# The last transform stage of a GFNet and MLP kernel: from 128-row groups to four quarters of the array

## The chip, the cores and the metric

The kernel runs on one core of a Trainium2 chip. The metric is the device time of that core in microseconds (us). A core has a matrix engine (PE, with its weight loads shown apart as PEld), a vector engine (DVE), a scalar engine (ACT), GpSimd (POOL), and SyncE (SP), which here issues most of the DMAs. PE reads both operands from SBUF and writes PSUM; a PSUM bank holds 512 fp32 values for each of 128 partitions.

## The reference

A Fourier mixing layer along the sequence, then an MLP with a hard-swish.

```python
X = np.fft.rfft(x, axis=1)                 # x: 8 x 3008 x 256
Y = X * (filt_r + 1j * filt_i)[None, :, :]
y = np.fft.irfft(Y, n=3008, axis=1)        # 24064 tokens of 256 channels in all
h = y @ w_in                               # 256 x 2048
g = h * np.clip(h + 3.0, 0.0, 6.0) / 6.0
out = g @ w_out                            # 2048 x 256
```

## The kernel before

**The transforms.** 3008 is 47 x 64, and each transform is done in two stages with the small tables of sines and cosines as matrix operands. For one batch element the units are: a_unit (47-point stage, stores to z_tmp), b_unit (64-point stage), f_unit and y_unit (multiplication by the filter, on DVE), bi_unit (inverse 64-point stage, stored to g_tmp by g_store), and the last stage, n_unit, which makes tokens out of g_tmp. The last stage writes channels on partitions and tokens along the free axis into `xn`, a ring of 768 token pairs, from which the MLP reads.

**The last stage.** Tokens come in pairs: from the real part of g_tmp comes the even sum (c = 0), from the imaginary part the odd sum (c = 1), and the two tokens of a pair are their sum and difference. For column j of the 64, the 47 even sums are a product over 48 rows (24 frequencies, twice: hh = 0 and 1), and so are the 47 odd sums. Columns are taken in chunks of NJ = 5, and there are 46 such chunks of full size over the 8 batch elements; columns 0 and 1 and the tail go in smaller ones. Before the change, the 5 x 48 = 240 rows of a chunk are stacked on 128 partitions in two layers of 128 and 112 rows, `t4[row, layer]`, and the table `groups` is block-structured to match: each layer multiplies 128 or 112 rows by 141 columns (three columns' worth, zero where a row isn't concerned), and the overlapping column of the two layers is summed in PSUM. `n_unit(i, dh)` does one 128-channel half dh of chunk i: four matmuls of 128 channels x 141 columns into one PSUM bank (L625), and one ACT copy into the ring (L641), two where the ring wraps. The unit is called twice a chunk, for dh = 0 and 1, in the same step or in two.

**Its loads.** `t4_load(i)` (L594) brings a chunk from g_tmp with SP: for each of five columns and two hh one DMA of 24 rows x 2 parts x 256 channels, one of them split at partition 128: 11 DMAs. `t4` has two slots of four layers, used in turn.

**The MLP.** It works on blocks of 512 tokens (256 pairs), 47 of them, with 8 steps a block (p = 0 to 7, 256 hidden units each), by a fast matrix multiplication with seven products instead of eight, in both matrices. One step holds 14 PE records of 256 columns (L690, up) and 28 of 128 columns (L766, down).

**What sets the order.** The order is written out by hand. The loop at the end walks over all steps. In each it issues up_1 (three products), then the early units planned for that step (`do(True)`: a_unit, b_unit, bi_unit, n_unit), then the rest of the MLP step, then the other planned work (`do(False)`: loads, stores, DVE work of the transforms). `plan` is filled by `at(step, fn, ...)`: the transforms of batch element n are spread over the blocks before the one where n begins, and each of these blocks has a kind, "c", "a", "A" or "B", by what it holds: a_units at steps 2, 4, 7 (c) and 1, 3, 5, 6, 7 (a); b_units at 2, 6 (A) and 4 (B); bi_units at 1 (c and the second A) and 0, 6 (B). `N_AT` gives for each kind the steps of the two n_units of a chunk that stands alone in its block, and of the first and second chunk where there are two. A chunk's load is planned one step after the second unit of the chunk before last.

**Banks.** a_unit, b_unit, bi_unit and n_unit draw their PSUM tiles from one pool of two banks, tag "f" (psF). a_unit, b_unit and bi_unit take both; an n_unit takes one. a_unit is also the model for what follows: it multiplies 47 rows by 64 columns on four quarters of the array, the two row halves (h) into a bank each, the two column halves (g) into 64 partitions each.

Of the kernel before, what the change touches and what calls it, by code (L numbers as in the profile page):

```python
# [10 lines left out]
FP32 = mybir.dt.float32  # L11
I32 = mybir.dt.int32
AXT = mybir.ActivationFunctionType
# [14 lines left out]
NA = 47  # L28
NC = 64
KH = 24  # L30
X0, XR = 16, 112
NF = N // 2 + 1
P = 128
D = 256
B = 8
DFF = 2048
HALF = 64
HC = NC // 2
# [9 lines left out]
TOK = 2 * NA  # L48
BLK = 512
NBLK = B * N // BLK  # L50
NJ = 5
PAIRS = BLK // 2
RING = 3 * PAIRS
ND = (NJ + 1) * TOK
NX = PAIRS - NJ * NA
NG = (HC - 2) // NJ
ATOM = 2 * KH
SPAN = 3 * NA
FIRST = tuple(range(NJ + 1, 0, -1))
LAST = NBLK - 1  # L60
CUT = NJ * 5 * NA + NA
# [17 lines left out]
def _make_tables():  # L79
    a = np.arange(NA)  # L80
    c = np.arange(NC)
    wa = np.zeros((P, HC * 2 * KH + 16))
    start = np.zeros((P, 2 * P))
    for h in range(2):
        for k in range(KH):
            th = 2 * np.pi * ((a * k) % NA) / NA

            at = k // 4 * 4 + (0, 2, 1, 3)[k % 4]
# [10 lines left out]
    for k in range(KH):  # L99
        for q in range(64):  # L100
            f, sign = (k + NA * q, 1.0) if q < 32 else (NA * (q - 31) - k, -1.0)
# [7 lines left out]
    for q in range(64):  # L109
        g, sign = (q, 1.0) if q < 32 else (31 - q, -1.0)  # L110
# [5 lines left out]
        at = g % 2 * 32 + (q // 2 if q < 32 else 16 + (q - 32) // 2)  # L116
# [8 lines left out]
        for h in range(2):  # L125
            s = -1.0 if h and g % 2 else 1.0
# [22 lines left out]

    rows = np.vectorize(row, excluded=(0, 1))  # L150
    late_rows = np.vectorize(late_row, excluded=(0, 1))
    groups = np.zeros((P, NG, 2, SPAN))
    ones = np.zeros((P, 2, TOK))
    first = np.zeros((P, NJ + 1, TOK))
    last = np.zeros((P, NJ + 1, TOK))
# [1 line left out]
    for k in range(KH):  # L157
        for j in range(HC):
            for (ri, hh), x in terms(k, j, rows).items():
                if j in FIRST:  # L160
                    first[hh * 64 + ri * 32 + k, FIRST.index(j)] = first_of(x, FIRST.index(j))
                if j < 2:
                    ones[ri * ATOM + hh * KH + k, j] = cs_of(x)
            if j in FIRST:
                for (ri, hh), x in terms(k, j, late_rows).items():
                    last[ri * ATOM + hh * KH + k, FIRST.index(j)] = cs_of(x)
            if j > 1:
                g, q = divmod(j - 2, NJ)
                c, s = (terms(k, j, rows)[0, hh][0] for hh in range(2))
                for hh, v in enumerate((c, s)):  # L170
                    t, p = divmod((NJ - 1 - q) * ATOM + hh * KH + k, P)
                    o = (NJ - 1 - q) * NA - t * 2 * NA
                    groups[p, g, t, o:o + NA] = v
        if k >= KH - TC:
            for q in range(64):
                fr = k + NA * q if q < 32 else NA * (q - 31) - k
                for n, j in enumerate(FIRST):
                    th = [2 * np.pi * ((fr * rows(j, h, a)) % N) / N for h in range(2)]
                    direct[q, k - KH + TC, n * TOK:(n + 1) * TOK] = 2 / N * first_of(np.cos(th), n)
                    direct[HALF + q, k - KH + TC, n * TOK:(n + 1) * TOK] = -2 / N * first_of(np.sin(th), n)  # L180
    wai = np.concatenate([t.reshape(P, -1) for t in (groups, ones, first, last)], axis=1)
    f = np.float32
# [4 lines left out]
def kernel(  # L187
# [9 lines left out]
    nc = tc.nc  # L197
# [12 lines left out]
    g_d = nc.dram_tensor("g_tmp", (B, NC, 2, KH, D), FP32, kind="Internal").ap()  # L210
# [6 lines left out]
    const = pool("const", 1)  # L217
# [14 lines left out]

    wa = const.tile([P, HC * 2 * KH + 16], FP32, name="wa")
    wf = const.tile([P, 4, 64], FP32, name="wf")
    NW = NG * 2 * SPAN + 2 * TOK
    wai = const.tile([P, NW], FP32, name="wai")
    groups = wai[:, 0:NG * 2 * SPAN].rearrange("p (g s n) -> p g s n", g=NG, s=2)
    ones = wai[:, NG * 2 * SPAN:].rearrange("p (s n) -> p s n", s=2)
    edge = wai[:, ds(2 * 2 * SPAN, ND)]
    edges = edge.rearrange("p (j n) -> p j n", n=TOK)  # L240
    wi = const.tile([P, 4, NC], FP32, name="wi")
    xs = const.tile([P, 3, XC, D], FP32, name="xs")
    ft = [const.tile([P, TC, D], FP32, name="ft%d" % i) for i in range(FB)]
    t4 = const.tile([P, 8, D], FP32, name="t4")
    xn = const.tile([P, 2, 2, RING], FP32, name="xn")
    w_all = const.tile([P, NP, 2, 7, P], FP32, name="w_all")
    w_in, w_out = ([w_all[:, p, i, :, :] for p in range(NP)] for i in range(2))
# [335 lines left out]
    def pair(i):  # L583
        b, js, o, n = chunks[i]
        return b * HC * NA + o, n
# [7 lines left out]

    def t4_load(i):  # L594
        b, js, _, _ = chunks[i]
        s0 = i % 2 * 4
        if len(js) < NJ:
            for q, j in enumerate(js):
                for hh in range(2):
                    for ri in range(2):  # L600
                        nc.sync.dma_start(t4[ds(ri * ATOM + hh * KH, KH), s0 + q, :], g_d[b, hh * HC + j, ri, :, :])
            return
        both = t4[:, ds(s0, 4), :].rearrange("p (c s) d -> p s c d", c=2)
        for q, j in enumerate(js):
            for hh in range(2):
                r, k = q * ATOM + hh * KH, 0
                while k < KH:
                    s_, p0 = divmod(r + k, P)
                    m = min(KH - k, P - p0)
                    nc.sync.dma_start(both[p0:p0 + m, s_, :, :],  # L610
                                      g_d[b, hh * HC + j, :, k:k + m, :].rearrange("ri k d -> k ri d"))
                    k += m

    ROWS = (P, NJ * ATOM - P)

    def n_unit(i, dh):
        ps = psF.tile([P, 512], FP32, name="psn", tag="f")
        b, js, o, n = chunks[i]
        s0 = i % 2 * 4
        t = b * HC * NA  # L620
        if len(js) == NJ:
            for c in range(2):
                for s_ in range(2):
                    r = ROWS[s_]
                    nc.tensor.matmul(ps[:, ds(c * NJ * NA + s_ * 2 * NA, SPAN)], t4[0:r, s0 + 2 * c + s_, ts(dh, P)],  # L625
                                     groups[0:r, (js[-1] - 2) // NJ, s_, :], start=c == 0 and s_ == 0, stop=True,
                                     skip_group_check=True)
            pieces = [(0, n, o, ps[:, 0:2 * n])]
        else:
            for q, j in enumerate(js):  # L630
                w = edges[0:2 * ATOM, FIRST.index(j), :] if i >= TAIL and j else ones[0:2 * ATOM, j, :]
                nc.tensor.matmul(ps[:, ts(q, TOK)], t4[0:2 * ATOM, s0 + q, ts(dh, P)], w, start=True, stop=True)  # L632
            pieces = [(a, m, to, ps[:, ts(q, TOK)])
                      for q, a, m, to in TO.get(i, [(q, 0, NA, o + q * NA) for q in range(len(js))])]
        for a, m_, to, src in pieces:
            src = src.rearrange("p (c n) -> p c n", c=2)
            done = 0
            while done < m_:
                r = (t + to + done) % RING
                m = min(m_ - done, RING - r)  # L640
                nc.scalar.activation(out=xn[:, dh, :, ds(r, m)], in_=src[:, :, ds(a + done, m)], func=AXT.Copy)  # L641
                done += m
        t += o
        if dh and (t + n) // PAIRS > t // PAIRS > 0:
            t_sums(t // PAIRS)


    def direct(i):
# [30 lines left out]
    def t_sums(k):  # L679
        t = xtp.tile([P, 5, PAIRS], FP32, name="xt")  # L680
        c0, s0, c1, s1 = (xb(k, d, c) for d in range(2) for c in range(2))
        u, v = (t[:, i, :] for i in (F5, F3))
        f1, f2, f3, f4, f5 = (t[:, i, :] for i in (F1, F2, F3, F4, F5))
        for o, x0, x1, op_ in ((f1, c0, s0, ALU.subtract), (u, c0, c1, ALU.add), (v, s0, s1, ALU.add),
                               (f4, u, v, ALU.subtract), (f5, u, v, ALU.add), (f2, c1, s1, ALU.add), (f3, f1, f2, ALU.add)):
            nc.gpsimd.tensor_tensor(out=o, in0=x0, in1=x1, op=op_)  # L686
        st["xt", k] = t
# [205 lines left out]
    plan = {}  # L893


    EARLY = (a_unit, b_unit, bi_unit, n_unit)

    def at(step, fn, *a):
        plan.setdefault((step, fn in EARLY), []).append((fn, a))

    with tc.manual_schedule():
# [126 lines left out]
                kinds[first[n] - 7 + d] = kind  # L1028

        N_AT = {"c": ((6, 6), (3, 3), (6, 6)), "a": ((2, 4), (2, 4), (6, 6)), "A": ((4, 5), (1, 1), (4, 5)), "B": ((2, 3), (1, 1), (2, 3))}  # L1030
        N_FIRST = {0: ((3, 4),), 1: ((), (2, 2), (3, 3)), 2: ((1, 1),), 3: ((1, 1),)}
        in_block = {}
        for i in range(2, len(chunks)):
# [2 lines left out]
        for i in range(2, len(chunks)):  # L1036
            k = pair(i)[0] // PAIRS
            head = chunks[i][2] == 0
            same = in_block[k]
            steps = (N_FIRST.get(k - 1) or N_AT[kinds.get(k - 1, "a")])[same.index(i) + 1 if len(same) > 1 else 0]  # L1040
            if head and len(same) == 1:
                steps = (6, 6)
            s0, s1 = ((k - 1) * NP + s for s in steps)
            n_at[i] = s1
            if head:
                stored = s0 - 3 + (k == first[1])
            at(max(stored, n_at[i - 2] + 1), t4_load, i)
            at(s0, n_unit, i, 0)
            at(s1, n_unit, i, 1)

# [136 lines left out]
```

## Time and profile before

| what | value |
|---|---|
| median of 3 runs | 2681.38 us (2681.22 to 2682.51) |
| the profiled execution: its own time | 2680.88 us |
| its span | 2679.1 us |
| granted TensorE clock | 1.00 of full speed |
| PE matmul records of L625 (n_unit, full chunks) | 736, mean 283 ns |
| ACT copies of L641, 128 x 470 | 62, mean 565 ns |
| DMAs of t4_load, 48 KB | 414 of the 418 in their group |

An fp32 matmul leaves two load records and two matmul records in the trace. "128\*128 128x141" means a stationary operand of 128 rows and 128 columns and a moving operand of 141 columns. Matmul durations reach from the start to a modelled end and overlap, so what a record costs is read from the distance between starts. A load (PEld) runs beside the matmul before it. In an instruction group, the figures after the bar are busy time and mean duration, and then the idle time of the engine just before them. In a list of waits, the figures are the total in us, the number of times, and the longest.

### The profile page before, as it was taken

Reading aid. Unit: us, or ns where it says so; the run is one execution under the profiler, and the core shown is the slowest. Engines: PE = TensorE matmul, PEld = TensorE weight load, DVE = VectorE, ACT = ScalarE, POOL = GpSimd, SP = SyncE. Lnnn points to the kernel's source line nnn. Section 1 sums busy time; section 2 is a strip of 40 time slices with the busy share of each in tenths; the row PEclk is TensorE's granted clock in tenths of the full one; section 3 lists DMA queues with packets and bytes.
Section 4 is the critical chain, followed back from the end, with each engine's and each line's share of the span. In section 5 each row is a group of like instructions: output and inputs, shape, how many; then the busy total and the mean of one; then the engine's idle time right before and its main releaser. Section 6 shows DMA issues by size and latency. Waiting matters only on the chain.

```text
span 2679.1 us, 48744 instructions
## 1 busy us (share of the span) xinstructions
PE 2661.1 (99%) x18640; PEld 2351.6 (88%) x18640; DVE 2069.1 (77%) x3503; ACT 1311.9 (49%) x2672; POOL 493.0 (18%) x731
## 2 busy tenths in 40 slices
PE   9999999999999999999999999999999999999999
PEld 6588898888988889888888888888888888899998
DVE  7878867887678876888777887788777878767666
ACT  3454454445444455445544545445454454554554
POOL 2251122111221112211121111211112111111110
PEclk9999999999999999999999999999999999999999
DMA  9632233212332123411233212231122321110000
GB/s 244 211 100 70 56 101 105 63 36 63 91 104 63 40 63 88 110 56 40 68 85 108 56 41 73 79 108 56 42 71 80 108 58 42 50 42 18 23 20 24
DMA packets 138663, 198.02 MB, mean 74 GB/s; under 512 B 27010, under 2 KB 102880, under 8 KB 138238
## 3 DMA queue, kind: packets, MB, share of 16 engines
q1 hardware_dynamic: 120901, 150.23, 19.6%
q0 software_dynamic: 16960, 44.16, 6.3%
q8 instruction: 148, 2.42, 0.4%
q14 instruction: 85, 0.70, 0.1%
q10 hardware_dynamic: 569, 0.50, 0.1%
HBM read 122.53 MB, written 83.98 MB: 77 GB/s over the span
## 4 chain that ended last, share of the span: by engine, by line
PE 94%; DVE 3%; DMA 2%; POOL 0%; issue 0%; ACT 0%; SPq 0%; POOLq 0%; DVEq 0%; ACTq 0%
PE po L766 43%; PE al L690 23%; PE be L690 17%; PE psn L625 3%; PE psf L543 2%; PE psf L452 2%; PE psf L499 1%; DVE g L740 1%; DMA g_tmp<-t 0%; DMA ft<-in_filt_i_dram 0%; DVE y L337 0%; DVE w_all L358 0%; DVE y L355 0%; PE psn L632 0%; DMA wa<-wb_t 0%
## 5 line engine op out<-in xcount | busy, mean ns | idle before, releaser
L766 PEld LDWEIGHTS po<-w_all,g 128*128 128x128 f32 x10276 | 1360.6, 191 | 149.1 <-issue 46.1
L766 PE MATMUL po<-w_all,g 128*128 128x128 f32 x10276 | 1397.6, 276 | 0.1
L735 ACT ACTIVATE r<-h,half_c 128x512 f32<-128x512 f32 x736 | 531.0, 721 | 342.3 <-DVE h L716 330.3
L740 DVE SCALAR_TENSOR_TENSOR g<-r,h 128x512 f32<-128x512 f32 x736 | 530.5, 721 | 198.0 <-ACT r L735 184.5
L690 PE MATMUL al<-xt,w_all 128*128 128x256 f32 x2208 | 659.9, 381 | 2.7 <-ACT s L701 1.4
L690 PE MATMUL be<-xt,w_all 128*128 128x256 f32 x1472 | 437.8, 379 | 0.0
L716 DVE TENSOR_TENSOR h<-be,s 128x512 f32<-128x512 f32 x368 | 253.8, 690 | 170.7 <-PE be L690 165.8
L690 PEld LDWEIGHTS al<-xt,w_all 128*128 128x128 f32 x2208 | 335.2, 192 | 4.5 <-ACT s L701 2.1
L690 PEld LDWEIGHTS be<-xt,w_all 128*128 128x128 f32 x1472 | 279.7, 190 | 37.9
L730 ACT ACTIVATE h<-al 128x256 f32<-128x256 f32 x368 | 141.3, 384 | 333.3 <-PE al L690 333.3
L721 DVE TENSOR_TENSOR h<-al,s 128x256 f32<-128x256 f32 x368 | 156.0, 424 | 157.7 <-PE al L690 156.5
L686 POOL TENSOR_TENSOR xt<-xn 128x256 f32<-128x256 f32 x184 | 153.8, 847 | 661.7 <-ACT xn L641 633.2
L748 DVE TENSOR_TENSOR g<-g 128x512 f32<-128x512 f32 x367 | 255.7, 697 | 12.6
L711 ACT ACTIVATE s<-al 128x256 f32<-128x256 f32 x368 | 141.4, 384 | 200.7 <-PE al L690 198.8
L702 ACT ACTIVATE s<-be 128x256 f32<-128x256 f32 x368 | 141.4, 384 | 174.6 <-PE be L690 174.6
L690 PE MATMUL al<-xn,w_all 128*128 128x256 f32 x736 | 220.8, 382 | 0.7 <-DVE h L721 0.6
L690 PE MATMUL be<-xn,w_all 128*128 128x256 f32 x736 | 219.0, 379 | 0.0
L750 DVE TENSOR_TENSOR g<-g 128x256 f32<-128x256 f32 x367 | 175.3, 478 | 12.5
L701 ACT ACTIVATE s<-al 128x256 f32<-128x256 f32 x368 | 141.2, 384 | 67.0 <-PE al L690 67.0
L747 DVE TENSOR_TENSOR g<-g 128x256 f32<-128x256 f32 x367 | 157.5, 429 | 12.5
L473 POOL DMA_DIRECT2D z_tmp<-t x192 | 95.1, 503 | 384.9 <-DVE t L466 366.8
L690 PEld LDWEIGHTS be<-xn,w_all 128*128 128x128 f32 x736 | 139.8, 190 | 19.1 <-DVE g L740 0.2
(149 smaller groups left out, 1844.0 us busy)
## 6 DMA issues: line engine op xcount, KB each, us to landing
g_tmp<-t POOLq DMA_DIRECT2D x96, 256.0 KB, 3.8
t<-z_tmp SPq DMA_DIRECT2D x42, 512.0 KB
t<-g_tmp SPq DMA_DIRECT2D x418, 48.0 KB
z_tmp<-t POOLq DMA_DIRECT2D x192, 96.0 KB, 2.6
xs<-in_x_dram SPq DMA_DIRECT2D x112, 128.0 KB
o_tmp<-o SPq DMA_DIRECT2D x46, 256.0 KB
ft<-in_filt_r_dram SPq DMA_DIRECT2D x168, 64.0 KB
ft<-in_filt_i_dram SPq DMA_DIRECT2D x168, 64.0 KB
```

The source lines that it names most:

```text
L686: nc.gpsimd.tensor_tensor(out=o, in0=x0, in1=x1, op=op_)
L690: nc.tensor.matmul(ps, w_in[p][:, w, :], x, start=start, stop=stop, skip_group_check=True)
L702: nc.scalar.activation(out=s5, in_=be[:, 1, :], func=AXT.Copy)
L711: nc.scalar.activation(out=s[:, 1, :], in_=al, func=AXT.Copy)
L716: nc.vector.tensor_tensor(out=st["h"][0].rearrange("p (a n) -> p a n", a=2), in0=be, in1=s, op=ALU.add)
L721: nc.vector.tensor_tensor(out=st["h"][1][:, 256:512], in0=al, in1=s5, op=ALU.add)
L735: nc.scalar.activation(out=r, in_=st["h"][i], func=AXT.Relu, bias=half_c, scale=1.0 / 6.0)
L740: nc.vector.scalar_tensor_tensor(out=st["g", k, p][:, o:o + 2, :].rearrange("p a n -> p (a n)"), in0=st["r", i], scalar=1.0, in1=st["h"][i ...
L747: v.tensor_tensor(out=g[:, G1, :], in0=g[:, G3, :], in1=g[:, G22, :], op=ALU.add)
L748: v.tensor_tensor(out=g[:, G3:G2 + 1:2, :], in0=g[:, G3:G1 + 1, :], in1=g[:, G11:G11 + 1, :].broadcast_to([P, 2, 256]), op=ALU.subtract)
L750: v.tensor_tensor(out=g[:, G4, :], in0=g[:, G12, :], in1=g[:, G2, :], op=ALU.subtract)
L766: nc.tensor.matmul(st["po", k][bank][:, part, u, :], g[:, a, ts(u, P)], w_out[p][:, w, :], start=(p == 0 and n in OPENS and u == 0), stop= ...
```

## The change

The 5 x 48 rows are no longer stacked over 128 partitions. The even part (c = 0) goes to partitions 0 to 47 and the odd part (c = 1) to partitions 64 to 111, one column j in each of five layers; `t4` has two slots of five layers. `groups` holds, for each j, the 48 x 47 table, once on each row half, with no zeros between. One unit, `n_five`, does a whole chunk, both 128-channel halves: for each column j, each half dh, each group g of 64 channels and each c, a matmul of 48 rows x 64 channels x 47 columns. Row half c and channel group g pick the quarter of the array; each c has a PSUM bank, in which the two dh lie side by side. Two ACT copies, one for each c, bring both halves into the ring. `n_unit` stays for the smaller chunks. `t4_load` brings a full chunk by four DMAs of 24 rows x 5 columns x 256 channels. `FIVE_AT` gives the one step of n_five for each kind of block.

```diff
-    groups = np.zeros((P, NG, 2, SPAN))
+    groups = np.zeros((P, HC, NA))
...
-                g, q = divmod(j - 2, NJ)
                 c, s = (terms(k, j, rows)[0, hh][0] for hh in range(2))
                 for hh, v in enumerate((c, s)):
-                    t, p = divmod((NJ - 1 - q) * ATOM + hh * KH + k, P)
-                    o = (NJ - 1 - q) * NA - t * 2 * NA
-                    groups[p, g, t, o:o + NA] = v
+                    groups[hh * KH + k, j] = groups[HALF + hh * KH + k, j] = v
...
-    t4 = const.tile([P, 8, D], FP32, name="t4")
+    t4 = const.tile([P, 2 * NJ, D], FP32, name="t4")
...
     def t4_load(i):
...
-        for q, j in enumerate(js):
-            for hh in range(2):
-                r, k = q * ATOM + hh * KH, 0
-                while k < KH:
-                    s_, p0 = divmod(r + k, P)
-                    m = min(KH - k, P - p0)
-                    nc.sync.dma_start(both[p0:p0 + m, s_, :, :],
-                                      g_d[b, hh * HC + j, :, k:k + m, :].rearrange("ri k d -> k ri d"))
-                    k += m
+        for c in range(2):
+            for hh in range(2):
+                j = hh * HC + js[0]
+                nc.sync.dma_start(t4[ds(c * HALF + hh * KH, KH), s0:s0 + NJ, :],
+                                  bass.AP(tensor=g_d.tensor, offset=g_d.offset + ((b * NC + j) * 2 + c) * KH * D,
+                                          ap=[[D, KH], [-2 * KH * D, NJ], [1, D]]))
...
+    def n_five(i):
+        b, js, o, n = chunks[i]
+        s0 = i % 2 * NJ
+        ps = [psF.tile([P, 512], FP32, name="psn", tag="f")[:, 0:2 * n].rearrange("p (e n) -> p e n", e=2) for c in range(2)]
+        for q, j in enumerate(js):
+            for dh in range(2):
+                for g in range(2):
+                    for c in range(2):
+                        r = ds(c * HALF, ATOM)
+                        nc.tensor.matmul(ps[c][ts(g, HALF), dh, ts(q, NA)], t4[r, s0 + q, ds(dh * P + g * HALF, HALF)],
+                                         groups[r, j, :], start=True, stop=True)
+        for c in range(2):
+            ring(i, 0, n, o, lambda at_: xn[:, :, c, at_], ps[c])
+        ready(i)
...
     def n_unit(i, dh):
...
-        if len(js) == NJ:
-            for c in range(2):
-                for s_ in range(2):
-                    r = ROWS[s_]
-                    nc.tensor.matmul(ps[:, ds(c * NJ * NA + s_ * 2 * NA, SPAN)], t4[0:r, s0 + 2 * c + s_, ts(dh, P)],
-                                     groups[0:r, (js[-1] - 2) // NJ, s_, :], start=c == 0 and s_ == 0, stop=True,
-                                     skip_group_check=True)
-            pieces = [(0, n, o, ps[:, 0:2 * n])]
...
-    EARLY = (a_unit, b_unit, bi_unit, n_unit)
+    EARLY = (a_unit, b_unit, bi_unit, n_unit, n_five)
...
         N_AT = {"c": ((6, 6), (3, 3), (6, 6)), "a": ((2, 4), (2, 4), (6, 6)), "A": ((4, 5), (1, 1), (4, 5)), "B": ((2, 3), (1, 1), (2, 3))}
+        FIVE_AT = {"c": (6, 3, 6), "a": (4, 2, 4), "A": (4, 0, 4), "B": (2, 1, 3)}
...
+            if five:
+                at(s1, n_five, i)
+                continue
             at(s0, n_unit, i, 0)
             at(s1, n_unit, i, 1)
```

`ring` is the old evacuation loop of n_unit with its wrap, and `ready` its last two lines (the call of t_sums, the POOL sums that prepare a block for the MLP), both made functions of their own.

More of the change, by code (lines that the diff above doesn't have):

```diff
@@ L55 @@
 NX = PAIRS - NJ * NA
-NG = (HC - 2) // NJ
 ATOM = 2 * KH
-SPAN = 3 * NA
 FIRST = tuple(range(NJ + 1, 0, -1))
@@ L234 @@
     wf = const.tile([P, 4, 64], FP32, name="wf")
-    NW = NG * 2 * SPAN + 2 * TOK
+    NW = HC * NA + 2 * TOK
     wai = const.tile([P, NW], FP32, name="wai")
-    groups = wai[:, 0:NG * 2 * SPAN].rearrange("p (g s n) -> p g s n", g=NG, s=2)
-    ones = wai[:, NG * 2 * SPAN:].rearrange("p (s n) -> p s n", s=2)
-    edge = wai[:, ds(2 * 2 * SPAN, ND)]
+    groups = wai[:, 0:HC * NA].rearrange("p (j n) -> p j n", n=NA)
+    ones = wai[:, HC * NA:].rearrange("p (s n) -> p s n", s=2)
+    edge = wai[:, ds(2 * (NJ + 1) * NA, ND)]
     edges = edge.rearrange("p (j n) -> p j n", n=TOK)
@@ L595, in t4_load @@
         b, js, _, _ = chunks[i]
-        s0 = i % 2 * 4
+        s0 = i % 2 * NJ
         if len(js) < NJ:
@@ L602, in t4_load, with ring, ready @@
             return
-        both = t4[:, ds(s0, 4), :].rearrange("p (c s) d -> p s c d", c=2)
-        for q, j in enumerate(js):
-            for hh in range(2):
-                r, k = q * ATOM + hh * KH, 0
-                while k < KH:
-                    s_, p0 = divmod(r + k, P)
-                    m = min(KH - k, P - p0)
-                    nc.sync.dma_start(both[p0:p0 + m, s_, :, :],
-                                      g_d[b, hh * HC + j, :, k:k + m, :].rearrange("ri k d -> k ri d"))
-                    k += m
-    ROWS = (P, NJ * ATOM - P)
+        for c in range(2):
[4 more added lines that the diff above has]
+                                          ap=[[D, KH], [-2 * KH * D, NJ], [1, D]]))
+    def ring(i, a, m_, to, out, src):
+        done = 0
+        while done < m_:
+            r = (chunks[i][0] * HC * NA + to + done) % RING
+            m = min(m_ - done, RING - r)
+            nc.scalar.activation(out=out(ds(r, m)), in_=src[:, :, ds(a + done, m)], func=AXT.Copy)
+            done += m
+    def ready(i):
+        t, n = pair(i)
+        if (t + n) // PAIRS > t // PAIRS > 0:
+            t_sums(t // PAIRS)
+    def n_five(i):
+        b, js, o, n = chunks[i]
+        s0 = i % 2 * NJ
+        ps = [psF.tile([P, 512], FP32, name="psn", tag="f")[:, 0:2 * n].rearrange("p (e n) -> p e n", e=2) for c in range(2)]
+        for q, j in enumerate(js):
+            for dh in range(2):
[7 more added lines that the diff above has]
+        ready(i)
     def n_unit(i, dh):
@@ L618, in n_unit @@
         b, js, o, n = chunks[i]
-        s0 = i % 2 * 4
-        t = b * HC * NA
-        if len(js) == NJ:
-            for c in range(2):
-                for s_ in range(2):
-                    r = ROWS[s_]
-                    nc.tensor.matmul(ps[:, ds(c * NJ * NA + s_ * 2 * NA, SPAN)], t4[0:r, s0 + 2 * c + s_, ts(dh, P)],
-                                     groups[0:r, (js[-1] - 2) // NJ, s_, :], start=c == 0 and s_ == 0, stop=True,
-                                     skip_group_check=True)
-            pieces = [(0, n, o, ps[:, 0:2 * n])]
-        else:
-            for q, j in enumerate(js):
[L631 to L645, printed above, removed]
+        for q, j in enumerate(js):
+            w = edges[0:2 * ATOM, FIRST.index(j), :] if i >= TAIL and j else ones[0:2 * ATOM, j, :]
+            nc.tensor.matmul(ps[:, ts(q, TOK)], t4[0:2 * ATOM, i % 2 * NJ + q, ts(dh, P)], w, start=True, stop=True)
+        for q, a, m, to in TO.get(i, [(q, 0, NA, o + q * NA) for q in range(len(js))]):
+            ring(i, a, m, to, lambda at_: xn[:, dh, :, at_], ps[:, ts(q, TOK)].rearrange("p (c n) -> p c n", c=2))
+        if dh:
+            ready(i)
     def direct(i):
@@ L1039 @@
             same = in_block[k]
-            steps = (N_FIRST.get(k - 1) or N_AT[kinds.get(k - 1, "a")])[same.index(i) + 1 if len(same) > 1 else 0]
+            at_, kind = same.index(i) + 1 if len(same) > 1 else 0, kinds.get(k - 1, "a")
+            steps = N_FIRST[k - 1][at_] if k - 1 in N_FIRST else (FIVE_AT[kind][at_],) * 2 if len(chunks[i][1]) == NJ else N_AT[kind][at_]
             if head and len(same) == 1:
@@ L1043 @@
             s0, s1 = ((k - 1) * NP + s for s in steps)
+            five = len(chunks[i][1]) == NJ
             n_at[i] = s1
```

## The prediction

> **What bounds the kernel now.** I read the page first, then the instruction groups kept apart by shape, then PE's waits, then PE's timeline around the units concerned.
>
> ```profile
> span 2679.1 us, 48744 instructions
> PE 2661.1 (99%) x18640; PEld 2351.6 (88%) x18640; DVE 2069.1 (77%) x3503; ACT 1311.9 (49%) x2672; POOL 493.0 (18%) x731
> PE 94%; DVE 3%; DMA 2%; POOL 0%; issue 0%; ACT 0%; SPq 0%; POOLq 0%; DVEq 0%; ACTq 0%
> ...
> L625 PE MATMUL psn<-wai,t 112*128 112x141 f32 x368 | 74.5, 283 | 0.0
> L625 PE MATMUL psn<-wai,t 128*128 128x141 f32 x368 | 74.3, 283 | 0.0
> ...
> PE al L948 <- ACT r L942: 2.8, 1, 2.8
> PE al L690 <- ACT s L701: 1.4, 2, 0.8
> ```
>
> PE is busy 99% of the span, carries 94% of the chain that ended last, and the dozen or so entries in its list of waits add up to about 11 us. PE is the bound: a nanosecond less on it is a nanosecond less in the span. The 736 records of L625 are 46 chunks of five columns, 16 records each: one fp32 matmul leaves two records (two passes). Their busy sums overlap, so I price by distance from start to start:
>
> ```profile
> 1353.79 0.59 PE L690 MATMUL be<-xt,w_all 128*128 128x256 f32 x2
> 1354.22 2.10 PE L625 MATMUL psn<-wai,t 128*128 128x141 f32 x16
> 1356.16 0.61 PE L766 MATMUL po<-w_all,g 128*128 128x128 f32 x4
> ...
> 1057.53 0.59 PE L690 MATMUL be<-xt,w_all 128*128 128x256 f32 x2
> 1058.05 1.09 PE L452 MATMUL psf<-xs,wa 47*64 47x256 f32 x16
> 1059.08 0.71 PE L766 MATMUL po<-w_all,g 128*128 128x128 f32 x4
> 1059.63 0.60 PE L690 MATMUL al<-xt,w_all 128*128 128x256 f32 x2
> ```
>
> The first three lines are one chunk today: 1356.16 - 1354.22 = 1.94 us for 16 records, 121 ns each, entered without a gap (1353.79 to 1354.22 is the normal 0.43 for two 256-column records). The last four are an a_unit, which already runs on four quarters of the array in the same order (row halves h, channel halves g). Two things are to be seen. Sixteen records of 256 columns take 1.03 us instead of 16 x 0.216 = 3.46: the quarters run together. And it is not free: L452 should start at 1057.53 + 0.43 = 1057.96 and starts 0.09 late; the four L766 records behind it occupy 0.55 (1059.08 to 1059.63) instead of 4 x 0.111 = 0.445. From 1057.96 to 1059.08 plus that 0.105 is 1.225 us; four groups of 0.216 are 0.864; entering and leaving the quarter mode costs 0.36 us.
>
> **What the Trainium skill says.** "TensorEngine Tiling (Array Packing)", Key Properties: changing the tiling mode drains TensorE, and different tiles can load weights and multiply in parallel. The trace agrees: 0.36 us a visit. The same page, Restrictions and Gotchas: different row tiles can't write one PSUM bank at a time; the change gives each row half its own bank, as a_unit does. "TensorE: Matmul & The Clock Gate", LDWEIGHTS: a load costs by its columns, columns / 1.2 ns, so 53 ns for 64. The trace shows it in the longest matmul durations, those of first matmuls whose load nothing covers:
>
> ```profile
> L499 PE MATMUL psf<-t,wf x16: 589/601/613, 1439.6 to 1440.1; 64*32 64x512 f32 x16
> ...
> L452 PE MATMUL psf<-xs,wa x896: 376/376/427, 80.6 to 2086.6; 47*64 47x256 f32 x180
> ...
> L766 PE MATMUL po<-w_all,g x9: 273/275/377, 1059.1 to 1060.9; 128*128 128x128 f32 x9
> ```
>
> 613 - 589 = 24 ns for 32 columns, 427 - 376 = 51 for 64, 377 - 275 = 102 for 128. Same page, "Wait — 56ns, not 53.3ns?": start to start is said never to drop below 25 ns, and to be 62 ns where instructions are decoded in software. That would decide this case, and is weighed below.
>
> **The change part by part.** All durations are from the profiled execution (2680.88 us, span 2679.1); the median shown is 2681.38, 0.5 above it.
>
> Removed: 46 x 16 records at 120.6 ns (mean over all L625 starts) = 1.93 us a chunk, 88.8 us.
>
> Added: a chunk becomes 5 columns x 2 x 2 x 2 = 40 matmuls, 80 records of 48 rows x 64 columns streaming 47: 20 groups of four quarters. The pitch of a group is the longer of two. Streaming: 256 columns go at 216 ns, 128 at 109, so 47 x 0.833 + 2.5 = 42 ns. Loading: in a_unit's single records the second pass's load in a quarter starts 55 ns after the first's; and where the kernel today streams only 94 columns against a 128-column load (L632, eight records in a row), starts are 112 ns apart and not the 81 of streaming, that is the 107 of a load plus 5, which for 64 columns is 58. So loading sets the pitch, 55 to 58; I take 57. Four loads of different quarters do run at once: in a_unit all four first matmuls show the same 51 ns exposed. A chunk is 20 x 0.057 + 0.36, less 0.02 because its last stream is shorter than its pitch: 1.48 us. Gain 0.45 a chunk.
>
> Does PE get its instructions fast enough? A group takes eight (four loads, four matmuls) in 57 ns, 7 ns each; break-even is where 20p + 0.34 = 1.93, p = 80 ns, 10 ns each. The trace bounds the supply indirectly. PE's semaphore instructions come 106 ns apart where two stand together (between the last two of a chunk today); with load, matmul, load, matmul between them, as in front of an a_unit, 125 ns. Four instructions cost 20 ns, 5 each. It is the thinnest argument here, since no stretch of the trace holds more than 16 such records.
>
> Moved: both channel halves now sit in one step and take both "f" banks. (a) The evacuations stay two ACT instructions of up to 470 elements (565 ns) a chunk, but both start after the last matmul; ACT's copy L711 then ends about 3.0 us behind the unit's due start, where PE's S3 product needs it at about 3.7. bi_unit has this very shape today and PE doesn't wait behind it. Cost nothing; without that slack 0.5 us a chunk. (b) Where the step before holds a second f_unit, the bank is freed only by DVE's L522, and the second matmul queues for it:
>
> ```profile
> 1147.56 0.69 DVE L522 TENSOR_TENSOR s<-psf,ft 64x512 f32<-64x512 f32 x1
> ...
> 1148.20 1.18 PE L543 MATMUL psf<-y,wi 64*64 64x512 f32 x8
> ```
>
> L522 ends at 1148.25 and the bi_unit takes 1.18 us instead of its usual 1.09: 0.09 us. The "A" blocks' step 4 meets this: about 12 chunks, 1.1 us. Behind an a_unit the sums of DVE end 0.97 us ahead of the slot: nothing. (c) Block 0 runs beside the weight conversion on DVE, and its chunk shares step 4 with an a_unit that needs both banks back: I count no gain for that chunk and 0.3 us of loss. (d) t4_load goes from 11 DMAs to 4 a chunk, the same 480 KB in 1 KB pieces. SP issues at some 0.37 us each and is about a third busy; it frees 2 to 3 us of SP a chunk, and the loads stay five or more steps ahead. Nothing. PE also meets fewer semaphore instructions, already hidden today. The tables are 96 KB shorter, hidden behind block 0.
>
> Sum: 45 x 0.45 = 20.1, less 1.1 and 0.3: 18.7. 2680.9 - 18.7 = 2662.2; on the median's footing 2662.7.
>
> **Rivals.** (1) Loads hidden better than I think, pitch 42: 20 x 0.042 + 0.36 = 1.20 a chunk, 33 us less: 2649. Against it stand the 112 ns of L632. (2) The gain is half eaten by waits: one more 0.2 us a visit, since both banks and all four loads of t4 must be there at the first matmul: 46 x 0.2 = 9 us, 2671. For it: every bank's release is now needed about 1 us earlier. Against: bi_unit and a_unit do the same with waits of at most 0.1. (3) Slower: PE's front end feeds 80 short record pairs no faster than the 25 ns that the skill gives as floor. A group is then 100 ns, a chunk 2.34 us, 46 x 0.41 = 19 us more: 2700. It decides from 20 ns a pair on; at 62 ns a pair a chunk is 5.3 us and the kernel takes 2836. For it: a_unit's 16 pairs could have stood in PE's queue beforehand, and 80 can't. Against: the 20 ns for four instructions. (4) Slower: the two channel halves of one row half can't go on loading at once, pitch 110: 2.54 a chunk, 28 us more, 2709. Against: b_unit's eight parts of 32 columns all show the same 24 ns.
>
> **How the numbers follow.** My forecast 0.68, rival 1 0.06, rival 2 0.12, rival 3 0.10, rival 4 0.04. A measurement of this kernel can tell 0.2% (5.4 us) from no change. Faster: 0.68 + 0.06 + 0.11 = 0.85; about 0.02 falls within 0.2%, from the edges of rivals 2 and 3; slower 0.13. The likeliest case with pitches of 55 to 58 and waits of 0 to 5 us gives 2659 to 2668. The range takes in rivals 1 and 2: 2649 to 2674; both slower rivals lie outside.
>
> **What would show it.** Twenty groups about 57 ns apart in each new unit, from the first matmul to the next L766 about 1.29 us; PE still at 99%; the be record ahead of a unit to its first matmul 0.09 late, as today for L452. Wrong if the matmuls of a unit bunch in the first 16 or so and then spread (rival 3), if the groups come 110 apart (rival 4), or if PE shows waits for L641, L522 or t4 in front of the new line (rival 2).

## The result and the profile after

| | before | after |
|---|---|---|
| median, 20 runs each | 2681.61 us | 2677.78 us |
| span of the profiled execution | 2679.1 us | 2676.8 us |

The ratio is 0.9986, 95% interval 0.9979 to 0.9993: 3.8 us faster, where 18.7 were forecast. Line numbers below are those of the changed kernel unless a unit of the old one is named; it is shorter by two lines in the MLP (L688 for L690, L719 for L721, L738 for L740, L764 for L766).

The page of the changed kernel, then its answer on the unit's tile, then the longest entries of PE's waits:

```profile
span 2676.8 us, 54235 instructions
PE 2646.1 (99%) x21584; PEld 2317.4 (87%) x21584; DVE 2062.9 (77%) x3503; ACT 1303.9 (49%) x2672; POOL 509.7 (19%) x731
PE 88%; DVE 8%; DMA 1%; issue 1%; ACT 0%; POOL 0%; SPq 0%; DVEq 0%; POOLq 0%; ACTq 0%
...
L628 PE MATMUL psn<-wai,t x3680: 230/232/254, 97.4 to 2493.0; 48*64 48x47 f32 x194
...
PE al L688 <- DVE h L719: 10.5, 25, 0.5
PE al L946 <- ACT r L940: 2.8, 1, 2.8
```

PE's share of the page hardly moves, but the chain does: DVE carried 3% of it before and carries 8% now. And a wait has come up that was nearly absent (0.6 us in three times before): PE's L688 for DVE's h.

The new unit itself is what was forecast. One of them in PE's timeline, and the step behind it:

```profile
787.35 0.59 PE L688 MATMUL be<-xt,w_all 128*128 128x256 f32 x2
787.87 1.48 PE L628 MATMUL psn<-wai,t 48*64 48x47 f32 x80
789.28 0.71 PE L764 MATMUL po<-w_all,g 128*128 128x128 f32 x4
789.83 0.60 PE L688 MATMUL al<-xt,w_all 128*128 128x256 f32 x2
...
798.17 1.05 PE L764 MATMUL po<-w_all,g 128*128 128x128 f32 x8
799.70 0.70 PE L688 MATMUL al<-xn,w_all 128*128 128x256 f32 x2 [0.47 <-DVE h L719]
800.23 0.49 PE L764 MATMUL po<-w_all,g 128*128 128x128 f32 x3
```

The unit takes 1.41 us from its first start to the next L764 (1.29 forecast; 1.31 measured in 33 of the 46 units, and 0.1 more here, where its second bank comes late). In the single records of an undisturbed unit its groups start 57 to 60 ns apart, after a first one of 80. Behind it, L688 at 799.70 should have followed the eight L764 records at 798.17 + 0.89 = 799.06; it starts 0.64 us late, and the next L764 follows after 0.53 us instead of 0.43, another 0.1.

The lengths of steps, taken from PE's single records as the distance between the first L688 starts of two steps, show the sum. This is block 18, an "A" block with one chunk, in us:

```
step             0     1     2     3     4     5     6     7
before         6.15  6.15  7.36  6.15  7.12  7.12  7.36  6.15
after          6.15  6.15  7.36  6.15  7.76  6.88  7.36  6.15
```

A step with the MLP alone takes 6.15. Half an old chunk added 0.97 to two steps; n_five adds 1.51 to one (1.61 here, with its late bank), so that 0.43 is won. But step 5, which has no unit left, takes 6.88 and not 6.15. So it is in the B blocks, where the pair of steps is 2 and 3. In the trace there are 21 such stalls, 20 of 0.73 us and one of 0.97: 15.6 us.

Why DVE is late is seen beside POOL. DVE's timeline of the changed kernel in steps 4 and 5 of the same block (number 12), then POOL's:

```profile
792.56 0.68 DVE L738 SCALAR_TENSOR_TENSOR g<-r,h 128x512 f32<-128x512 f32 x1
793.27 1.10 DVE L526 TENSOR_TENSOR y<-s 64x512 f32<-64x512 f32 x1
794.41 1.10 DVE L527 TENSOR_TENSOR y<-s 64x512 f32<-64x512 f32 x1
795.62 1.03 DVE L738 SCALAR_TENSOR_TENSOR g<-r,h 128x512 f32<-128x512 f32 x1
796.69 0.83 DVE L745 TENSOR_TENSOR g<-g 128x256 f32<-128x256 f32 x1
797.56 0.69 DVE L746 TENSOR_TENSOR g<-g 128x512 f32<-128x512 f32 x1
798.28 0.42 DVE L748 TENSOR_TENSOR g<-g 128x256 f32<-128x256 f32 x1
798.62 0.68 DVE L714 TENSOR_TENSOR h<-be,s 128x512 f32<-128x512 f32 x1
...
790.49 2.10 POOL L684 TENSOR_TENSOR xt<-xn 128x256 f32<-128x256 f32 x3 [19.56 <-ACT xn L610]
792.67 2.29 POOL L684 TENSOR_TENSOR xt<-xt 128x256 f32<-128x256 f32 x2
794.93 1.17 POOL L684 TENSOR_TENSOR xt<-xn 128x256 f32<-128x256 f32 x1
796.18 1.06 POOL L684 TENSOR_TENSOR xt<-xt 128x256 f32<-128x256 f32 x1
```

From 790.5 to 797.2 POOL does the seven sums of t_sums, which start as soon as the chunk's evacuation is in the ring. Beside them DVE's y_unit (L526, L527) takes 1.10 us each and L738 1.03. L714 is reached at 798.62, and L719 behind it is what PE waits for. In the kernel before, the same stretch reads:

```profile
793.04 0.69 DVE L531 TENSOR_TENSOR y<-s 64x512 f32<-64x512 f32 x1
793.77 0.69 DVE L532 TENSOR_TENSOR y<-s 64x512 f32<-64x512 f32 x1
794.56 0.69 DVE L740 SCALAR_TENSOR_TENSOR g<-r,h 128x512 f32<-128x512 f32 x1
...
797.56 0.69 DVE L716 TENSOR_TENSOR h<-be,s 128x512 f32<-128x512 f32 x1 [0.66 <-PE be L690]
798.81 0.42 DVE L721 TENSOR_TENSOR h<-al,s 128x256 f32<-128x256 f32 x1 [0.56 <-PE al L690]
799.15 1.24 DVE L740 SCALAR_TENSOR_TENSOR g<-r,h 128x512 f32<-128x512 f32 x1
...
789.71 0.82 POOL L686 TENSOR_TENSOR xt<-xn 128x256 f32<-128x256 f32 x1 [18.66 <-ACT xn L641]
796.82 1.41 POOL L686 TENSOR_TENSOR xt<-xn 128x256 f32<-128x256 f32 x2 [6.29 <-ACT xn L641]
```

There DVE waits for PE (0.66 and 0.56), not PE for DVE, although it is busy for 6.53 of the 7.12 us of step 4. Only one of the sums could run in step 4, because the ring got its second channel half in step 5. The sums stretch DVE there too (L740 1.24), but step 5 held 0.97 us of n_unit on PE to cover it. And L716 takes its 0.69 although POOL is at work: it has one operand in PSUM. That is what the Trainium skill has in "SBUF — State Buffer", Who interferes with whom: a DVE instruction with two SBUF inputs contends with a GpSimd instruction that reads SBUF; one with at most one SBUF input does not, outside the 2-port performance modes (which a tensor_tensor, by the same section, doesn't have). The trace agrees, with 0.69 going to 1.10 for the first sort and 0.69 staying for the second.

### The profile page after: what moved, and what is told of

It reads as the page before. It is cut to its first block, busy times and chain, and to the rows that moved or that the text cites. A ratio compares the mean times of both kernels' runs of the same rounds, so it can differ in the third digit from the quotient of the medians.

```text
span 2676.8 us, 54235 instructions
## 1 busy us (share of the span) xinstructions
PE 2646.1 (99%) x21584; PEld 2317.4 (87%) x21584; DVE 2062.9 (77%) x3503; ACT 1303.9 (49%) x2672; POOL 509.7 (19%) x731
## 3 DMA queue, kind: packets, MB, share of 16 engines
q1 hardware_dynamic: 117037, 150.12, 19.8%
## 4 chain that ended last, share of the span: by engine, by line
PE 88%; DVE 8%; DMA 1%; issue 1%; ACT 0%; POOL 0%; SPq 0%; DVEq 0%; POOLq 0%; ACTq 0%
PE po L764 40%; PE al L688 22%; PE be L688 16%; PE psn L628 2%; PE psf L538 2%; PE psf L447 2%; DVE g L738 2%; PE psf L494 1%; DVE y L526 1%; DVE y L527 1%; DVE g L745 1%; DVE h L714 1%; DVE h L719 1%; DVE g L746 1%; DMA w_all<-in_x_dram 1%
## 5 line engine op out<-in xcount | busy, mean ns | idle before, releaser
L764 PEld LDWEIGHTS po<-w_all,g 128*128 128x128 f32 x10276 | 1361.2, 191 | 154.7 <-issue 44.1
L764 PE MATMUL po<-w_all,g 128*128 128x128 f32 x10276 | 1402.5, 277 | 0.4 <-DVE g L738 0.2
L738 DVE SCALAR_TENSOR_TENSOR g<-r,h 128x512 f32<-128x512 f32 x736 | 526.7, 716 | 209.8 <-ACT r L733 195.6
L688 PE MATMUL al<-xt,w_all 128*128 128x256 f32 x2208 | 660.0, 381 | 3.7 <-ACT s L699 2.4
L688 PE MATMUL be<-xt,w_all 128*128 128x256 f32 x1472 | 437.9, 379 | 0.0
L714 DVE TENSOR_TENSOR h<-be,s 128x512 f32<-128x512 f32 x368 | 253.8, 690 | 166.5 <-PE be L688 161.7
L688 PEld LDWEIGHTS al<-xt,w_all 128*128 128x128 f32 x2208 | 335.2, 192 | 5.5 <-ACT s L699 3.0
L688 PEld LDWEIGHTS be<-xt,w_all 128*128 128x128 f32 x1472 | 279.7, 190 | 37.9
L719 DVE TENSOR_TENSOR h<-al,s 128x256 f32<-128x256 f32 x368 | 155.8, 423 | 153.5 <-PE al L688 152.4
L684 POOL TENSOR_TENSOR xt<-xn 128x256 f32<-128x256 f32 x184 | 144.6, 805 | 548.4 <-ACT xn L610 548.4
L688 PE MATMUL al<-xn,w_all 128*128 128x256 f32 x736 | 222.6, 384 | 10.5 <-DVE h L719 10.5
L688 PE MATMUL be<-xn,w_all 128*128 128x256 f32 x736 | 219.0, 379 | 0.0
L554 POOL DMA_DIRECT2D g_tmp<-t x96 | 55.6, 593 | 648.1 <-ACT t L541 648.1
L699 ACT ACTIVATE s<-al 128x256 f32<-128x256 f32 x368 | 140.9, 383 | 67.3 <-PE al L688 67.3
```

Of the source, the lines that this page charges most:

```text
L688: nc.tensor.matmul(ps, w_in[p][:, w, :], x, start=start, stop=stop, skip_group_check=True)
L714: nc.vector.tensor_tensor(out=st["h"][0].rearrange("p (a n) -> p a n", a=2), in0=be, in1=s, op=ALU.add)
L719: nc.vector.tensor_tensor(out=st["h"][1][:, 256:512], in0=al, in1=s5, op=ALU.add)
L738: nc.vector.scalar_tensor_tensor(out=st["g", k, p][:, o:o + 2, :].rearrange("p a n -> p (a n)"), in0=st["r", i], scalar=1.0, in1=st["h"][i ...
L764: nc.tensor.matmul(st["po", k][bank][:, part, u, :], g[:, a, ts(u, P)], w_out[p][:, w, :], start=(p == 0 and n in OPENS and u == 0), stop= ...
```

## The experiments

Three theories were tried. Each diff is against the changed kernel, or against the kernel before where the old unit is named; "..." stands for what is left out. (1) The sums of t_sums have moved beside the first y_unit and make DVE late. (2) The second y_unit step has lost its work on PE, and DVE's y alone runs over. (3) The new unit's form, with both banks evacuated at its end, delays ACT and DVE. The medians of before in these sets are 2681.2 to 2681.6 us.

**The old unit, both halves in the first step.**

```diff
-  ... "A": ((4, 5), (1, 1), (4, 5)), "B": ((2, 3), (1, 1), (2, 3))}
+  ... "A": ((4, 4), (1, 1), (4, 4)), "B": ((2, 2), (1, 1), (2, 2))}
```

> The kernel before, with both halves of n_unit in the first of the two y_unit steps of A and B blocks (A: 4,4 for 4,5; B: 2,2 for 2,3). Same matmuls as before. Theory 1 (POOL's seven sums of t_sums now start a step early, beside the first y_unit, stretch DVE's SBUF-to-SBUF instructions from 0.69 to 1.1 us, and DVE is late for L716/L721 in the next step) and theory 2 (the second y_unit step has lost its n_unit, so PE runs into DVE there): about 22 waits of 0.7 us on DVE's h, near 2695 us. Theory 3 (the wait comes from the new unit's form: both banks evacuated at its end): no such waits, 2681 us.

Measured 2693.03 us, ratio 1.0043 (1.0028 to 1.0058). Steps 4 and 5 of block 18 take 8.09 and 6.69: the old unit stalls in the same place. Theory 3 falls. The stall is 0.54 in the A blocks and 0.2 to 0.55 in the B blocks instead of 0.73, hence 2 us under the figure. The old pair keeps PE longer in step 4 (8.09 for 7.76), which gives DVE time; I take this for the reason.

**n_five in the second y_unit step.**

```diff
-  ... "A": (4, 0, 4), "B": (2, 1, 3)}
+  ... "A": (5, 0, 5), "B": (3, 1, 3)}
```

> The changed kernel with n_five in the second y_unit step (A: 5 for 4, B: 3 for 2). Theory 1: the sums start beside the second y_unit, and DVE is late in a step after the y_units, where it has slack; the waits go, 2661 to 2666 us. Theory 2: the first y_unit step is now the bare one, the waits move there, 2676 to 2680 us. Theory 3: waits stay behind the unit, 2676 to 2680 us.

Measured 2668.26 us, ratio 0.9951 (0.9936 to 0.9966); once more in the last set, for comparison:

> e2 once more, on the same chip as e7, for the comparison: 2667 to 2669 us.

Measured 2668.28 us (0.9938 to 0.9963). Ten us come back by moving the unit one step. Step 4, now bare, takes 6.34, step 5 7.66. So theory 2 is right for 0.19 us of the first y_unit step in A blocks and not for the 0.73. The result is 2 us above what theory 1 gave; 0.18 us is lost in steps 0 and 6 of most B blocks too (7.63 for 7.45), where DVE, still behind after the stretched steps, frees the second bank of a bi_unit later (L538 takes 1.35 us there, the same unit 1.18 before).

**The sums held back by two steps.** The unit stays where the change put it; only POOL waits.

```diff
...
-    def t_sums(k):
+    def t_sums(k, after=None):
         t = xtp.tile([P, 5, PAIRS], FP32, name="xt")
+        if after is not None:
+            nc.gpsimd.tensor_tensor(out=t[:, F1, :], in0=after, in1=after, op=ALU.add)
...
+                late = kind in "AB" and k - 1 not in N_FIRST and s1 % NP in (2, 4)
+                at(s1, n_five, i, late)
+                if late:
+                    at(s1 + 2, ready, i, s1 + 2)
```

> The changed kernel, n_five where it was, but in A and B blocks POOL's sums are held back by one more POOL add that reads DVE's G4 of two steps on, so they run after both y_units (one add of 0.73 us more on POOL, its result overwritten). Theory 1: the waits on DVE's h go, 2661 to 2666 us. Theory 2 and theory 3: the unit's place and form are unchanged, the waits stay, 2676 to 2680 us.

Measured 2672.36 us, ratio 0.9965 (0.9953 to 0.9978). Between the two hunks shown, n_five leaves out its call of `ready` where `late` is set. The same stretch of DVE and, behind it, the added POOL instruction (the lines of the MLP lie three further on here, L741 for L738):

```profile
797.07 0.68 DVE L741 SCALAR_TENSOR_TENSOR g<-r,h 128x512 f32<-128x512 f32 x1
797.78 0.69 DVE L526 TENSOR_TENSOR y<-s 64x512 f32<-64x512 f32 x1
798.50 0.69 DVE L527 TENSOR_TENSOR y<-s 64x512 f32<-64x512 f32 x1
...
801.78 0.61 POOL L681 TENSOR_TENSOR xt<-g 128x256 f32<-128x256 f32 x1 [32.48 <-DVE g L751]
```

With POOL silent until 801.78, y_unit is back at 0.69 and step 5 takes 6.15 us, although it is bare. This is the cleanest of the runs: PE's work and its order are those of the changed kernel, only the time of POOL's sums differs (and one POOL add is new), and all of the 0.73 goes. What is left over 2666 is small waits where the sums now run: 0.17 in step 7 of A blocks and in step 5 of B blocks, 0.3 in steps 0 and 6 of B blocks.

**The sums held back by one step.** As before with `s1 + 1`.

> As e3, but the sums are held back by one step only, so that they start inside the second y_unit step, as in the kernel before. Theory 1: the second y_unit is the one stretched; the step after it holds a b_unit on PE and no y_unit, so no or few waits: 2661 to 2670 us. Theory 2 and theory 3: 2676 to 2680 us.

Measured 2687.44 us, ratio 1.0022 (1.0012 to 1.0032). Theory 1 as I had put it was wrong here. Step 5 is clean (6.15), but steps 6 and 7 take 7.83 and 6.65 for 7.36 and 6.15: two waits instead of one. A b_unit on PE is no shelter, because f_unit brings DVE more than 2 us in each of these steps (L515 to L517, 0.69 each). In block 12 DVE is busy for 7.07 of the 7.83 us of step 6 and for 6.00 of the 6.65 of step 7. I read this so: what counts is DVE's whole load over the steps in which the sums run, the stretching with it, against PE's length of the same steps. No run tries that rule by itself.

**Away from the y_units.** n_five where DVE has no transform work.

```diff
-  ... "A": (4, 0, 4), "B": (2, 1, 3)}
+  ... "A": (0, 0, 1), "B": (1, 1, 3)}
```

> The changed kernel with n_five in A and B blocks at the steps where DVE has no transform work (A: 0,0,1 for 4,0,4; B: 1,1,3 for 2,1,3), so that POOL's sums run there. Theory 1: the unit's own gain of 18 us comes through, no waits on h: 2661 to 2665 us, below e2. Theory 2 (y_units with no other PE work in their step run over): both y_unit steps of every A and B block are now bare, about twice the waits of the changed kernel: near 2692 us.

Measured 2669.61 us, ratio 0.9957 (0.994 to 0.9974), 5 to 8 above the figure of theory 1 and far from that of theory 2. The stalls on h are gone, but the first A block of each batch element has a new one: its step 1 takes 6.73, because PE's L764 starts 0.45 us late for DVE's L840. The MLP's own last sums of the block before fall into the same steps. It is DVE's load again, of another origin.

**The old unit at the same steps.**

```diff
-  ... "A": ((4, 5), (1, 1), (4, 5)), "B": ((2, 3), (1, 1), (2, 3))}
+  ... "A": ((0, 0), (0, 0), (1, 1)), "B": ((1, 1), (1, 1), (3, 3))}
```

> The kernel before with its n_units at the steps of e5. It separates the place from the unit. Theory 1: the old unit has almost nothing to gain from the place (the kernel before waits some 1.4 us in all on DVE's h in these blocks): 2679 to 2682 us, so that the distance to e5 is the unit's own 17 to 19 us. Theory 2: some 2710 us.

Measured 2685.46 us, ratio 1.0016 (1.001 to 1.0023), 4 above what I gave: for the old unit these places are a little worse than its own. At equal places the new unit is worth 2685.46 - 2669.61 = 15.9 us, near the 17 to 19 expected.

**The places mixed.** Step 1 for the first A block of a batch element, 0 for the second, 1 for B blocks; the first A block gets a kind of its own, X.

```diff
-        for d, kind in enumerate("caABAB"):
+        for d, kind in enumerate("caXBAB"):
...
-  ... "A": (4, 0, 4), "B": (2, 1, 3)}
+  ... "A": (0, 0, 5), "X": (1, 0, 1), "B": (1, 1, 3)}
```

> The changed kernel with n_five placed for DVE in each kind of block: first A block of a batch at step 1 (with two chunks 0 and 1), second A block at 0 (0 and 5), B blocks at 1 (1 and 3). In e5 the first A block lost 0.45 us in its step 1, where L764 waited for DVE's o L840, and e2 lost 0.18 us in steps 0 and 6 of B blocks. Theory 1: both go, 2665 to 2668 us, at or under e2. If the sums cost wherever they run, 2669 or more, like e5.

Measured 2666.19 us, ratio 0.9943 (0.993 to 0.9957): 15.0 us under before, 11.6 under the changed kernel's median, and 2.1 under e2 in the same set. It is the fastest version of the study, from five runs. Block 18 reads 6.15, 7.66, 7.36, 6.15, 6.35, 6.15, 7.36, 6.15: the unit costs its 1.51 in step 1, and only the 0.2 of the bare step 4 is lost. Most B blocks lose 0.1 to 0.3 in their step 2.

**Eighths of the array.** e2 with 32 channels a matmul, to try the supply of instructions, the thinnest argument of the prediction.

```diff
-                for g in range(2):
+                for g in range(4):
...
-  ... ps[c][ts(g, HALF), dh, ts(q, NA)], t4[r, s0 + q, ds(dh * P + g * HALF, HALF)],
+  ... ps[c][ts(g, 32), dh, ts(q, NA)], t4[r, s0 + q, ds(dh * P + g * 32, 32)],
```

> e2 with 32 channels a matmul in place of 64: eight parts of the array instead of four, 160 records a chunk in 20 groups of eight. [...]If the load alone sets the pitch of 58 ns, groups come 42 to 47 ns apart and a chunk is 0.2 to 0.3 us shorter, near 2657 us. If PE takes no more than one instruction in 5 ns, sixteen take 80 ns, and a chunk is 0.4 us longer, near 2686 us.

Measured 2714.79 us from two runs, ratio 1.0125 (1.0106 to 1.0143): 46.5 us over e2. In the 31 units that run through, the groups of eight start 46 to 120 ns apart, 72 on average, although the load is down to half. Sixteen instructions in 72 ns are 4.5 ns each, next to the 5 read off before. The first three intervals are 46 to 60 ns and only then longer, so the array itself can go faster than 72. What holds it there was not tried further. And there is worse. PE's waits of this kernel, then from its page the DMA queue that is marked "instruction" (packets, MB, share of the 16 DMA engines):

```profile
PE psn L628 <- issue: 21.7, 17, 3.6
PE al L946 <- ACT r L940: 2.8, 1, 2.8
...
q8 instruction: 199, 3.26, 0.5%
```

Seventeen times PE stands inside the unit, up to 3.6 us, and the list of waits names no one. The trace has it beside that queue: each of the 17 stops ends 1.3 to 1.6 us after the end of one of its packets of 16 KB, of which there is one in 14 us on average. So PE was waiting for its next instructions, as near as a trace can show it. The queue brings 148 packets in the kernel before, 170 in the changed kernel and 199 here, which grows with PE's instructions, by one packet for some 250 to 270 of them. The changed kernel, with half as many instructions a unit, has no such stop. In four stretches of 3.4 to 6.8 us the granted clock is 0.5 besides; three of them begin within 1.2 us of the end of the three stops of over 3 us. Of the 46.5 us the slower pace is some 12 (46 x 0.27 in the length of a step), the stops are 22, and half of 17 us at half the clock is some 8; these three are estimates from the profiled execution.

## Why the prediction was wrong

**What bounds the kernel: right.** PE does; what is taken from it shows in the span unless another engine becomes late.

**The unit: right, to a few per cent.** 1.48 us a chunk was forecast; steps lengthen by 1.51 where nothing disturbs (7.66 - 6.15), against 1.94 for two old halves. The pitch is the one read off for the load: 58 to 59 ns, where I took 57 out of 55 to 58, and not the 42 of the stream. No run shows the load alone as its cause, since e8 met another limit. Entering and leaving cost 0.36 as read off a_unit. The gain of the unit is 46 x 0.43 = 19.8 us (20.7 forecast). Supply of instructions held, at 7 ns each. e8's 4.5 fits the 5 read off from the semaphore intervals, but not the stops: with twice the instructions a unit they cost more than the unit had won. (The prediction's 45 x 0.45 is 20.25 and not 20.1, which decides nothing.)

**The late bank (b): right.** Step 4 of A blocks takes 7.76, 0.1 over 7.66. **Block 0 (c): too little.** Block 1 starts 0.6 us later than before, where no gain and a loss of 0.3 were put down.

**The step that failed is "Moved".** I listed what the merged unit's place does to ACT's copies, to the banks, to block 0 and to t4_load, and priced all of it at 1.4 us. Two things that move with the second half were left out. The call of t_sums at the end of the unit starts seven POOL instructions, and they now run one step earlier. And the 0.97 us of PE work that the second half put into the second y_unit step went away, without my asking who was using that time: DVE was. e3 shows the first by itself (hold the sums back and the stall is gone), e1 shows that it isn't the new unit. The second is argued from the kernel before, where the sums stretch DVE in step 5 and PE doesn't wait; no run gives the cover back alone. A bare step alone costs nothing in e3 and 0.19 us in the A blocks of e2. Together the two cost 15.6 us in 21 stalls.

The sum, in spans: -19.8 for 46 units; +15.6 for the stalls; +1.2 for twelve late banks; -1.4 for five waits of 0.28 us of the kernel before, in "a" blocks, that are gone; -0.7 in step 1 of block 32, where a bi_unit stood directly behind a whole old chunk and took 1.80 us instead of 1.09; +2.6 in blocks 0 to 3, 1.0 of it in block 0 and 0.9 where PE waits for ACT's L699 in block 1 (the causes there were not followed up). That makes -2.5; the spans differ by 2.3. That the total is near nothing is chance: a gain and a loss of like size from different causes.

**Rival 2 was the nearest case, with the wrong mechanism.** Its case was that waits eat half of the gain. They ate four fifths, but not through the banks or t4: through DVE, which stood at 77% busy on the page. An average of 77% hid steps in which DVE was nearly full: in block 12 of the kernel before it is busy for 6.53 of the 7.12 us of step 4 and for 5.61 of the 6.15 of steps 3 and 7. The lines L520 to L522, L531 and L740 of those steps would have shown it.

**Rivals 1, 3 and 4** didn't occur: pitch neither 42, nor 100, nor 110. The 25 ns from start to start, which rival 3 took as a floor, doesn't show between quarters: within a group the four matmuls start 5 to 8 ns apart.

## What to carry to other kernels

When work is merged or moved in a schedule written out by hand, list what it releases as well as what it issues: the next engine's work starts with it, and whatever ran under its old place loses its cover. Check the engine that isn't the bound step by step, not by its share of the span. And where POOL and DVE both read two SBUF operands, as here, their times add in part (0.69 to 1.10 us for DVE, 0.73 to 1.1 for POOL): place POOL's bursts where DVE is waiting anyway.

## What was not expected of the hardware

- DVE instructions with two SBUF operands (128 x 512, 64 x 512 fp32) take 1.03 to 1.24 us instead of 0.69 while POOL's sums run, and POOL's own sums up to 1.2 instead of 0.73; with one operand in PSUM DVE keeps its 0.69.
- PE takes instructions at about 4.5 ns each over 320 of them (e8), and in 15 of 46 such units stops for up to 3.6 us, until 1.3 to 1.6 us after a packet of the instruction queue has ended. With 160 instructions a unit, at 7 ns each, it never does.
- Quarter-array matmuls of 47 columns start in groups of four every 58 ns, the pitch that was read off for a 64-column load, and not the 42 of their stream.
